# Query projections, VectorE priorities and dummy products in the head of a one-core transformer block

## The chip, the cores and the metric

The kernel runs on one core of a Trainium2 chip. The metric is device time in microseconds (us). The runs of one kernel scatter by a few us. A ratio is the mean time of one kernel's runs over the mean of the other's runs of the same rounds, with a 95% interval, so it is not quite the ratio of the medians that are quoted.

In this kernel TensorE multiplies matrices (15918 products before the change), ScalarE computes exponentials and tanh (1024 and 112), and VectorE (1498 instructions) copies results out of PSUM, adds and normalises. "Span" is the length of the profiled execution. It is about 2 us shorter than the time of the same run (before: 1158.1 and 1159.92 us).

## The reference, cut to what matters

```python
# x: 2048 x 1024, 32 heads of 32, one shared key/value head, FFN width 3584
mod = (silu(c) @ w_mod).reshape(...)             # six vectors of 1024: sa, ca, ga, sb, cb, gb
h = layernorm(x) * (1 + ca) + sa
q, k, v = h @ wq, h @ wk, h @ wv                 # softmax(q k' / sqrt(32)) @ v, then @ wo
x = x + ga * attention(h)
h = layernorm(x) * (1 + cb) + sb
x = x + gb * ((silu(h @ w1) * (h @ w3)) @ w2)
```

## The kernel before

The program is a list of nodes with dependencies. A list scheduler in the kernel file places them when it is built, using its own estimates of durations, and then writes one fixed instruction order for each engine. Queries are worked on in 8 blocks of 256. For each of 8 groups of 4 heads, a "score group" (line 915) writes scores for 256 keys, and two exponentials (line 925) read them. P·V (line 975) and row sums (line 1002) follow. The FFN of the block before fills TensorE between score groups. For the first block only, the projections of head groups 0 to 3 (`HEAD = 4`) and half of the keys are done first, so that exponentials can start early. This beginning is called the head below.

```python
# the scheduler's choice among ready nodes: lowest key first
if e == "pe":                                    # TensorE
    def key(c):
        s, n = c
        if n.cls == "S":   r = 0                 # score groups
        elif n.cls is not None: r = 1 if att or t - n.est > 1.0 else 4     # P·V, row sums
        else:              r = 3 if n.prio >= 4 else 0.5
        return (r, n.prio, n.seq)
elif e == "dve":                                 # VectorE
    def key(c):
        s, n = c
        p = n.prio
        if t - n.est > 4.0: p -= 3
        return (p, n.seq)

# "warm": if the schedule sees TensorE idle before 250 us, it inserts k dummy products
gap = s - t_free[e] - 0.3 - (0.1 if mode != "F" else 0.0) - (0.1 if n.mode != "F" else 0.0)
k = int(gap / self.warm[1])

def ln(t):                                       # layer norm of one tile of 128 tokens
    (ln_stats_act if t in ONACT else ln_stats)(t)        # ln_stats has priority 2 - bp
    ln_scale(t, 1)
    ln_norm(t, t, en="pool" if t in ONPOOL else "dve")   # priority 2 - bp, bp = 0

# transposes of norm tiles have priority TRP = 1; a projection's default is prio=5
kproj(0, 256, (2, 3, 4, 5, 6, 7))                # third argument: allowed PSUM banks
qproj(0, 256, 0, (2, 3, 4, 5, 6, 7), prio=1)
kproj(256, 256, (2, 3, 4, 5, 6, 7))
kproj(512, 512, (1,))
...
qproj(0, 256, 1, (0, 1))
vproj(0, (0, 1))
vproj(1, (0, 1))
for f in range(2, HEAD):
    qproj(0, 256, f, (0, 1))
tr(8, 4, (0, 1))                                 # transposes of tiles 8 to 11
for t in range(12, 16):
    ln(t)
... # cut
# attention: score group i uses four of the six score banks, which are banks 2 to 7
parts = [(0, 2, 2 * ((2 * i) % 3), 2), (2, 2, 2 * ((2 * i + 1) % 3), 2)]
```

The softmax here doesn't subtract the row's maximum and nothing guards it: scores larger than these inputs give would overflow.

## Time and profile before

| | before |
|---|---|
| time, median of the first 3 runs | 1160.13 us (1158.57 to 1160.46) |
| span of the profiled run | 1158.1 us |
| first exponential | 29.2 us |
| ScalarE idle for scores, 28 to 130 us | 12.3 us, of which 0.5 is before the first exponential |
| last score group starts | 1044.7 us |
| from there to the end ("tail") | 113.4 us |

First come the busy times by stretch: from:to, length, busy us of TensorE (PE), its weight loads (PEld), VectorE (DVE), ScalarE (ACT) and GpSimd with instruction counts, then TensorE's granted clock, the DMA share and GB/s.

```profile
18.50:25.30 6.80, 6.71 (x114) 6.00 (x115) 1.88 (x4) 4.05 (x9) 0.00 (x0) 0.50 1.07 364
39.00:46.00 7.00, 5.67 (x104) 3.63 (x106) 6.01 (x18) 5.97 (x7) 4.08 (x10) 0.51 0.41 117
46.00:60.00 14.00, 11.16 (x261) 8.29 (x254) 11.27 (x34) 9.27 (x10) 0.99 (x2) 1.00 0.34 89
600.00:700.00 100.00, 99.60 (x1407) 67.44 (x1406) 94.25 (x137) 99.88 (x115) 1.73 (x2) 1.00 0.63 177
```

In the middle (600 to 700 us) ScalarE is hardly ever idle (99.88 of 100 us). In the head it is: between 46 and 60 us it works 9.3 of 14 us. Twice the clock is granted at half (0.50 and 0.51 in the first two stretches). Finer stretches put the two half-clock intervals at 18.5 to 25.3 us and 39.0 to 45.8 us, 6.8 us each. Why the clock falls there is not shown.

ScalarE's idle times in the head, from its timeline: start, us, what ran, and in brackets the idle time before it and what ended that.

```profile
29.21 3.83 ACT L925 ACTIVATE UREG<-SP 128x1024 bf16<-128x1024 f32 x4 [0.49 <-PE SP L915]
35.60 7.44 ACT L925 ACTIVATE UREG<-SP 128x1024 bf16<-128x1024 f32 x8 [2.56 <-PE SP L915]
43.80 1.94 ACT L925 ACTIVATE UREG<-SP 128x1024 bf16<-128x1024 f32 x2 [0.76 <-PE SP L915]
47.02 9.27 ACT L925 ACTIVATE UREG<-SP 128x1024 bf16<-128x1024 f32 x10 [1.29 <-PE SP L915]
61.86 13.44 ACT L925 ACTIVATE UREG<-SP 128x1024 bf16<-128x1024 f32 x14 [5.57 <-PE SP L915]
```

The longest, 5.57 us, is explained by TensorE's own timeline: after the score group at 53.60 it transposes, does two rounds of P·V and row sums, and only then the fourth query projection (59.67), which the score group at 61.41 needs.

```profile
53.60 0.40 PE L915 MATMUL SP<-QT,KT 32*128 32x256 bf16 x8 [0.77 <-ACT UREG L925]
...
56.06 1.06 PE L975 MATMUL PB<-UREG,V 128*32 128x256 bf16 x32
56.95 1.05 PE L1002 MATMUL PB<-UREG,SEL 128*32 128x256 bf16 x32
57.82 1.04 PE L975 MATMUL PB<-UREG,V 128*32 128x256 bf16 x32
...
58.69 1.05 PE L1002 MATMUL PB<-UREG,SEL 128*32 128x256 bf16 x32
59.67 1.05 PE L658 MATMUL PB<-HREG,WREG 128*128 128x256 bf16 x8
...
61.41 0.40 PE L915 MATMUL SP<-QT,KT 32*128 32x256 bf16 x8
```

A projection has rank 3 on TensorE (priority 5), a transpose rank 0.5 (priority 1). Norms that VectorE finishes early make transposes ready, and these pass the fourth projection (`f = 3`).

The third projection (`f = 2`) was late before any of these transposes (the first runs at 48.52 us). It needs a PSUM bank (projections and values share banks 0 and 1), and VectorE emptied the values (line 651) only at 40.52 us, after norm statistics (line 530):

```profile
37.57 2.46 DVE L530 BATCH_NORM_STATS2 ST<-X 128x6 f32<-128x512 bf16 x4
40.52 0.44 DVE L651 TENSOR_TENSOR V<-PB,VB 128x128 bf16<-128x128 f32 x2
41.76 1.44 PE L658 MATMUL PB<-HREG,WREG 128*128 128x256 bf16 x6
```

The cause is the ageing rule in the cut above: work that has waited for over 4 us gets 3 points off its priority, so an aged norm (2 - 3 = -1) passes an evacuation (1).

The chain of work that ended last, by engine:

```profile
PE 92%; ACT 3%; DVE 3%; DMA 1%; SPq 1%; issue 0%; POOL 0%; DVEq 0%
```

This is not to be read as "TensorE alone is the limit". In the middle TensorE and ScalarE are both busy almost all the time (99.60 and 99.88 us of the 100 us from 600 to 700), and the chain follows one of them by hairs.

### The profile page before, as it was taken

The page shows a single profiled execution, that of the slowest core. Times are in us where ns is not written, and L with a number is a line of the kernel's source. Part 1 is how long each engine was busy: PE and PEld are TensorE (multiplying, and loading weights), DVE is VectorE, ACT ScalarE, POOL GpSimd, SP SyncE. Part 2 cuts the span into 40 slices and gives each one's busy share as a digit, 9 for nine tenths or more (in the row PEclk, how much of TensorE's full clock was granted, in tenths as well). Part 3 has the DMA queues.
Part 4 walks back from the last instruction along what each step waited for, and adds up shares of the span by engine and source line. Part 5 has one row for each costly group of instructions (what it writes and reads, how often), then busy time and mean ns, then how long its engine had stood idle before and what let it go on. Part 6 is the DMA issues. An engine that isn't in the chain of part 4 may idle for free.

```text
span 1158.1 us, 35702 instructions
## 1 busy us (share of the span) xinstructions
PE 1122.6 (97%) x15918; PEld 767.1 (66%) x15918; DVE 984.7 (85%) x1498; ACT 1027.6 (89%) x1170; POOL 43.5 (4%) x86
## 2 busy tenths in 40 slices
PE   7799998999979999999999999999999999999998
PEld 6564444776646766777577766776677766777887
DVE  5837889999888999899999998999989999997452
ACT  5789999999999999999999999999999999992110
POOL 3200001000000001000100001000100010000000
PEclk8899999999989999999999999999999999999999
DMA  9337005956546565856496567766586649756996
GB/s 331 113 129 220 19 2 127 275 169 178 166 122 190 169 193 149 248 170 192 119 279 196 159 177 194 226 169 174 152 252 181 185 122 258 204 152 192 284 291 160
DMA packets 385417, 211.10 MB, mean 182 GB/s; under 512 B 21744, under 2 KB 376048, under 8 KB 385264
## 3 DMA queue, kind: packets, MB, share of 16 engines
q1 hardware_dynamic: 383184, 208.69, 64.5%
q8 instruction: 125, 2.05, 0.8%
q10 hardware_dynamic: 2080, 0.13, 0.1%
q14 instruction: 28, 0.23, 0.1%
HBM read 201.46 MB, written 4.19 MB: 178 GB/s over the span
## 4 chain that ended last, share of the span: by engine, by line
PE 92%; ACT 3%; DVE 3%; DMA 1%; SPq 1%; issue 0%; POOL 0%; DVEq 0%
PE PB L1141 33%; PE PB L1175 16%; PE SP L915 14%; PE PB L975 11%; PE PB L1107 5%; PE PB L658 4%; PE SP L1141 3%; ACT UREG L925 3%; PE SP L1175 2%; PE PB L1002 2%; DMA UREG<-in_w_mod_dram 1%; PE PB L637 1%; PE PB L838 0%; PE SP L1107 0%; DVE WO L850 0%
## 5 line engine op out<-in xcount | busy, mean ns | idle before, releaser
L925 ACT ACTIVATE UREG<-SP 128x1024 bf16<-128x1024 f32 x1024 | 968.6, 1075 | 18.8 <-PE SP L915 16.4
L948 DVE TENSOR_TENSOR UREG<-UREG 128x2048 bf16<-128x2048 bf16 x240 | 292.8, 1220 | 12.8 <-ACT UREG L925 10.8
L915 PE MATMUL SP<-QT,KT 32*128 32x256 bf16 x4096 | 204.8, 274 | 16.0 <-ACT UREG L925 15.0
L1141 PE MATMUL PB<-QT,WREG 128*128 128x256 bf16 x1648 | 207.4, 274 | 1.8 <-DVE DSB L1026 1.6
L1141 PEld LDWEIGHTS PB<-QT,WREG 128*128 128x128 bf16 x1648 | 150.1, 98 | 46.8 <-issue 31.2
L942 DVE TENSOR_TENSOR UREG<-UREG 128x2048 bf16<-128x2048 bf16 x120 | 146.4, 1220 | 11.5 <-PE PB L1002 6.4
L915 PEld LDWEIGHTS SP<-QT,KT 32*128 32x128 bf16 x4096 | 61.2, 93 | 138.6 <-ACT UREG L925 79.6
L1141 PE MATMUL PB<-QT,HREG 128*128 128x256 bf16 x1056 | 133.7, 274 | 0.8 <-DVE DSB L1026 0.8
L975 PE MATMUL PB<-UREG,V 128*32 128x256 bf16 x4032 | 132.2, 277 | 1.7 <-DVE QT L610 0.9
L975 PEld LDWEIGHTS PB<-UREG,V 128*32 128x32 bf16 x4032 | 99.3, 98 | 27.5 <-issue 17.9
L1141 PEld LDWEIGHTS PB<-QT,HREG 128*128 128x128 bf16 x1056 | 96.1, 98 | 29.7 <-issue 19.6
L1175 PE MATMUL PB<-WREG,HREG 128*128 128x256 bf16 x812 | 101.2, 273 | 0.0
L1175 PEld LDWEIGHTS PB<-WREG,HREG 128*128 128x128 bf16 x812 | 75.3, 98 | 20.4 <-issue 11.4
L1175 PE MATMUL PB<-HREG 128*128 128x256 bf16 x532 | 67.8, 274 | 0.0
L1141 PE MATMUL PB<-QT,X 128*128 128x256 bf16 x528 | 67.8, 274 | 0.0
L658 PE MATMUL PB<-HREG,WREG 128*128 128x512 bf16 (+1 forms) x312 | 64.1, 343 | 0.3 <-DVE DSB L1026 0.3
L957 DVE TENSOR_TENSOR UREG<-UREG 128x2048 bf16<-128x2048 bf16 x52 | 63.4, 1220 | 0.5
L1150 ACT ACTIVATE GSB<-GSB 128x512 bf16<-128x512 bf16 x56 | 38.8, 693 | 27.5 <-DVE GSB L1148 27.5
L1014 DVE COPY XN<-PB 128x256 f32<-128x256 f32 x63 | 26.6, 422 | 39.6 <-PE PB L1002 39.3
L1175 PEld LDWEIGHTS PB<-HREG 128*128 128x128 bf16 x532 | 49.2, 98 | 14.3 <-issue 8.0
L1107 PE MATMUL PB<-WO,QT 128*128 128x512 bf16 x232 | 57.6, 381 | 0.2 <-DVE QT L661 0.2
L1141 PEld LDWEIGHTS PB<-QT,X 128*128 128x128 bf16 x528 | 48.2, 98 | 14.3 <-issue 9.3
(139 smaller groups left out, 1031.9 us busy)
## 6 DMA issues: line engine op xcount, KB each, us to landing
WREG<-in_B_w_dram SPq DMA_DIRECT2D x112, 512.0 KB, 5.1
HREG<-in_B_w_dram SPq DMA_DIRECT2D x74, 512.0 KB, 5.2
WREG<-in_B_w_dram SPq DMA_DIRECT2D x33, 896.0 KB, 5.1
X<-in_B_w_dram SPq DMA_DIRECT2D x38, 512.0 KB, 5.1
HREG<-in_B_w_dram SPq DMA_DIRECT2D x21, 896.0 KB, 5.2
X<-in_B_w_dram SPq DMA_DIRECT2D x10, 896.0 KB, 5.1
X<-in_A_x_dram SPq DMA_DIRECT2D x32, 256.0 KB, 5.0
WREG<-in_w_mod_dram SPq DMA_DIRECT2D x16, 512.0 KB, 4.7
```

The costliest lines, as they stand in the source:

```text
L658: g = mm_group(NC, lambda e, b, c: e.matmul(b[:, 0:n], WQ[:, c, f * P:(f + 1) * P], HT[:, c, sl], start=c == 0, stop=c == NC - 1), lambda ...
L915: r = e.matmul(SP[:, b, o:o + qn], KT[32 * gg:32 * gg + 32, kts[j] * P:(kts[j] + 1) * P], QT[32 * gg:32 * gg + 32, f, q0:q0 + qn], start=T ...
L925: G.add("act", lambda e, u=u, h0=h0, n=n, b0=b0, nb=nb: e.activation(U[:, u, h0 * W:(h0 + n) * W].rearrange("p (b w) -> p b w", b=nb), SP[ ...
L942: G.add("dve", lambda e, tr=tr, u=u, fu=first_u: e.tensor_tensor(TR[:, tr, 0:4 * W], U[:, fu, 0:4 * W], U[:, u, 0:4 * W], ALU.add), reads= ...
L948: G.add("dve", lambda e, tr=tr, u=u: e.tensor_tensor(TR[:, tr, 0:4 * W], TR[:, tr, 0:4 * W], U[:, u, 0:4 * W], ALU.add), reads=[("TR", tr) ...
L957: G.add("dve", lambda e, ta=ta, tb=tb: e.tensor_tensor(TR[:, ta, 0:4 * W], TR[:, ta, 0:4 * W], TR[:, tb, 0:4 * W], ALU.add), reads=[("TR", ...
L975: r = e.matmul(PB[g.bank][32 * gg:32 * gg + 32, 0:qn], V[:, kt, :], U[:, pu, (gg * npk + j) * qn:(gg * npk + j + 1) * qn], start=w0 + n == ...
L1014: G.add("dve", lambda e, g=g, f=f: e.tensor_copy(ASB[:, f % 4, 0:qn], PB[g.bank][:, 0:qn]), writes=[("ASB", f % 4), ("XN", 2 + f % 4 // 2) ...
L1107: g = mm_group(NC, lambda e, b, f, t=t, h=h: e.matmul(b, QT[:, f, t * P:(t + 1) * P], WO[:, f, h * 512:(h + 1) * 512], start=f == 0, stop= ...
L1141: return e.matmul(b[:, j * qn:(j + 1) * qn], w13[:, w, c, j * P:(j + 1) * P], QT[:, c, q0:q0 + qn], start=c == 0, stop=c == NC - 1)
L1150: G.add("act", lambda e, b=b: e.activation(TB[b], GS[b], ACT.Tanh, scale=0.5), reads=[("GS", b)], writes=[("TB", b)], clear=alias("TB") if ...
L1175: G.add("pe", lambda e, g=g, j=j, fc=fc, hf=hf, first=first, w2s=w2s: e.matmul(PB[g.bank][:, j * 256:(j + 1) * 256], HHT[:, hf * NH + fc, ...
```

## The change

The intent is to have the queries of the first four head groups earlier, to let VectorE empty PSUM before it works on norms that are not yet needed, and to keep TensorE's clock up in the first 26 us (it was granted at 0.50 from 18.5 to 25.3 us). That the new dummies do this was my assumption.

```diff
-                gap = s - t_free[e] - 0.3 - (0.1 if mode != "F" else 0.0) - ...
+                gap = s - t_free[e] - (0.05 if t < self.warm[4] else 0.3) - (0.1 if mode != "F" else 0.0) - ...
@@ vproj: evacuation of the values
-              writes=[("V", tb)], groups=[(g, "r")], dur=dve_t(128), prio=1)
+              writes=[("V", tb)], groups=[(g, "r")], dur=dve_t(128), prio=-4)
@@ qproj: evacuation of the queries
-              writes=qkeys(f, t0, n), ..., prio=-5 if t0 == f == 0 else 1)
+              writes=qkeys(f, t0, n), ..., prio=-5 if t0 == 0 and f < HEAD else 1)
@@ ln
-        (ln_stats_act if t in ONACT else ln_stats)(t)
+        bp = -3 if t >= 8 else 0
+        if t in ONACT:
+            ln_stats_act(t)
+        else:
+            ln_stats(t, bp=bp)
         ln_scale(t, 1)
-        ln_norm(t, t, en="pool" if t in ONPOOL else "dve")
+        ln_norm(t, t, en="pool" if t in ONPOOL else "dve", bp=bp)
@@ sequence and banks
-    kproj(0, 256, (2, 3, 4, 5, 6, 7))
-    qproj(0, 256, 0, (2, 3, 4, 5, 6, 7), prio=1)
-    kproj(256, 256, (2, 3, 4, 5, 6, 7))
-    kproj(512, 512, (1,))
+    kproj(0, 256, (2, 3, 4, 5))
+    qproj(0, 256, 0, (2, 3, 4, 5), prio=1)
+    kproj(256, 256, (6, 7))
+    kproj(512, 512, (6, 7))
 ... # cut
-    qproj(0, 256, 1, (0, 1))
+    qproj(0, 256, 1, (0, 1), prio=1)
     vproj(0, (0, 1))
+    qproj(0, 256, 2, (0, 1), prio=1)
     vproj(1, (0, 1))
-    for f in range(2, HEAD):
-        qproj(0, 256, f, (0, 1))
+    for f in range(3, HEAD):
+        qproj(0, 256, f, (0, 1), prio=1)
@@ dummies: 128 columns become 512
-                r = e.matmul(PB[b][:, 0:P], IDENT[:], IDENT[:], ...)
+                r = e.matmul(PB[b], IDENT[:], IDENT[:].unsqueeze(1).broadcast_to([P, 4, P]), ...)
-    G.warm = (WARM, P / 2400.0 + 0.0026, warm, ident)
+    G.warm = (WARM, MM, warm, ident, 26.0)
```

The change has three parts, named below by what they are: the **sequence** (with its banks), the **priorities** on VectorE and the **dummies**.

(The diff is shortened.)

More of the change, by code (lines that the diff above doesn't have):

```diff
@@ L227, in schedule @@
             if e == "pe" and self.warm is not None and t < self.warm[0]:
-                gap = s - t_free[e] - 0.3 - (0.1 if mode != "F" else 0.0) - (0.1 if n.mode != "F" else 0.0)
+                gap = s - t_free[e] - (0.05 if t < self.warm[4] else 0.3) - (0.1 if mode != "F" else 0.0) - (0.1 if n.mode != "F" else 0.0)
                 fb = [x for x in free_banks() if x[0] + SEM_LAT <= t_free[e]]
@@ L662, in qproj @@
               reads=[("BIA", 0 if f == 0 else 1 if f < HEAD else 2)],
-              writes=qkeys(f, t0, n), groups=[(g, "r")], dur=dve_t(n), prio=-5 if t0 == f == 0 else 1)
+              writes=qkeys(f, t0, n), groups=[(g, "r")], dur=dve_t(n), prio=-5 if t0 == 0 and f < HEAD else 1)
     def qkeys(f, q0, qn):
@@ L1215, in f @@
             for _ in range(k):
-                r = e.matmul(PB[b][:, 0:P], IDENT[:], IDENT[:], start=True, stop=True, skip_group_check=True)
+                r = e.matmul(PB[b], IDENT[:], IDENT[:].unsqueeze(1).broadcast_to([P, 4, P]), start=True, stop=True, skip_group_check=True)
             return r
         return f
-    G.warm = (WARM, P / 2400.0 + 0.0026, warm, ident)
+    G.warm = (WARM, MM, warm, ident, 26.0)
     span = G.schedule(range(8))
```

## The prediction

> **What bounds the kernel now.** From its first exponential (29.2 us, timeline) to its last (about 1041 us) ScalarE sets the pace: in the stretches table it is 99.5% busy in nearly every 100 us between 200 and 1000, one exponential of 128x1024 each 0.93 us, 1024 of them, plus about 0.46 us for each of 98 tanh. Between two score groups (1.86 us) TensorE has 1.75 us of work (0.33 us of scores, 13 products of 0.109 us). After the last score TensorE alone works for about 117 us (450 L1141, 448 L1175 and the last block). So 29.2 + 952 + 45 + 12 (ScalarE idle in the head) + 117 = 1155, against a span of 1158.
>
> The change touches only the first 62 us directly. There, by the waits and the timeline, ScalarE idles four times between exponentials: 2.56 us (33.0), 0.76 (43.0), 1.29 (45.7) and 5.57 (56.3): 10.2 us in all. The last is TensorE doing transposes, P·V and row sums of two groups (3.9 us) and only then the fourth query projection, which the next score needs. The clock was granted at half from 18.5 to 25.3 and from 39.0 to 45.8.
>
> **What it does, from the instruction order.**
> 1. Query projections 1 to 3 come before score groups 3, 5 and 6 instead of 3, 8 and 13; their evacuations pass the norms on VectorE. Summing the trace's durations over the new TensorE order, the 7.0 us between score groups 12 and 13 disappears; no later gap of the head exceeds 2.5 us. The waits of 0.76, 1.29 and 5.57 us should fall to under 1 us together: -7 us.
> 2. It costs something: the key projections of 512 columns now sit in score banks. The second score group comes after 28 key products, query projection 1 and half the first values: 4.25 us after the first, where ScalarE has 1.86 us of work. I expect a ScalarE wait of about 2.3 us near 31 us, about what the old 2.56 us was (1.4 us of which was TensorE stopped in mid-group with nothing to wait for).
> 3. Dummies: 133 of 128 columns become 54 of 512. The first run takes the same time (56x128 against 15x512 columns). In 15.1 to 18.5 they add only about 0.2 us of streaming. [...]both half-clock stretches here are 6.8 us[...]. Whether 0.2 us tips it at 18.5 I hold for even odds. If it does, 0 to 1.3 us is gained before the first exponential, because w_mod still arrives at DMA pace to 21 us or later. Expected: -0.5 us. The second cold stretch should vanish[...].
> 4. One tanh less precedes the last exponential: -0.5 us.
> 5. Given back: FFN work is reordered too. After the last score 482 first-FFN products remain instead of 450, 32 x 0.109 = +3.5 us in the tail where only TensorE works.
>
> Sum: -7 -0.2 -0.5 -0.5 +3.5 = about -4.7 us.
>
> **Prediction: 1155.5 us, 1150 to 1160 us.** Faster by over 2%: 0.01; within: 0.98; slower: 0.01.
>
> **Right if** ScalarE's idle time on scores between 28 and 130 us falls from 12.3 to about 5 us, its longest wait is the second score group's, first exponential within 1.5 us of 29.2, last exponential 7 to 9 us earlier, and the stretch from last score to end is 3 to 4 us longer.
>
> **Wrong if** VectorE is late with the tighter evacuations so that TensorE's fixed order stalls; if the mid-group stop moves into a score's path; if a cold stretch appears elsewhere; or if the tail is not purely TensorE's, so that the 3.5 us does not return.

## The result, and the profile after

The changed kernel took 1155.89 us (median of 6, 1155.31 to 1157.44) beside 1159.47 us for the kernel before (6 runs). The ratio is 0.9972, interval [0.9959, 0.9984]: faster, by a third of a per cent. Line numbers move by five: 915 is now 920, 925 is 930, 1175 is 1180.

The same stretches after:

```profile
18.50:25.30 6.80, 6.17 (x166) 4.76 (x164) 2.05 (x8) 4.59 (x11) 0.83 (x1) 1.00 1.06 363
39.00:46.00 7.00, 5.30 (x104) 2.62 (x104) 7.00 (x20) 7.00 (x9) 2.31 (x6) 1.00 0.51 143
46.00:60.00 14.00, 12.00 (x260) 7.69 (x256) 9.00 (x25) 14.00 (x16) 1.44 (x4) 1.00 0.91 299
600.00:700.00 100.00, 99.05 (x1407) 67.48 (x1404) 94.59 (x138) 99.59 (x114) 2.24 (x4) 1.00 0.64 178
```

In this profile the clock stays up (1.00 from 13 to 55 us), and ScalarE is busy without a break from 39 to 60 us. Its timeline now has one long wait:

```profile
27.79 1.91 ACT L930 ACTIVATE UREG<-SP 128x1024 bf16<-128x1024 f32 x2
33.66 29.51 ACT L930 ACTIVATE UREG<-SP 128x1024 bf16<-128x1024 f32 x32 [3.96 <-PE SP L920]
63.54 1.94 ACT L930 ACTIVATE UREG<-SP 128x1024 bf16<-128x1024 f32 x2 [0.37 <-PE SP L920]
65.72 9.43 ACT L930 ACTIVATE UREG<-SP 128x1024 bf16<-128x1024 f32 x10 [0.25 <-PE SP L920]
```

That wait stands before the second score group, as predicted, but it is longer: 3.96 us instead of 2.3. Between the first score group (27.03 us) and the second (33.21 us) TensorE stopped for 1.24 us in the middle of a group, with nothing to wait for ("issue"):

```profile
27.36 0.39 PE L637 MATMUL SP<-HREG,WKS 128*32 128x512 bf16 x1
28.99 0.40 PE L637 MATMUL SP<-HREG,WKS 128*32 128x512 bf16 x3 [1.24 <-issue]
```

The other end of the kernel shows what was given back. Here are the last score group and TensorE's last group, before:

```profile
1044.74 0.40 PE L915 MATMUL SP<-QT,KT 32*128 32x256 bf16 x8
1147.42 6.28 PE L1175 MATMUL PB<-WREG,HREG 128*128 128x256 bf16 x56
```

and after:

```profile
1036.41 0.40 PE L920 MATMUL SP<-QT,KT 32*128 32x256 bf16 x8
1142.81 6.28 PE L1180 MATMUL SP<-WREG,HREG 128*128 128x256 bf16 x56
```

The last score group comes 8.3 us earlier (1044.74 - 1036.41). From there to the end of the span it is 1158.1 - 1044.74 = 113.4 us before and 1153.5 - 1036.41 = 117.1 us after, so 3.7 us go back. 8.3 - 3.7 = 4.6 us is the difference of the spans.

The chain of work that ended last has changed sides, although the time fell by a third of a per cent only:

```profile
PE 46%; ACT 45%; DVE 6%; issue 1%; SPq 1%; DMA 1%; POOL 0%
```

### The profile page after: what moved, and what is told of

It reads as the page before. It is cut to its first block, busy times and chain, and to the rows that moved or that the text cites. A ratio compares the mean times of both kernels' runs of the same rounds, so it can differ in the third digit from the quotient of the medians.

```text
span 1153.5 us, 35455 instructions
## 1 busy us (share of the span) xinstructions
PE 1119.9 (97%) x15839; PEld 762.4 (66%) x15839; DVE 989.5 (86%) x1498; ACT 1026.0 (89%) x1170; POOL 39.0 (3%) x86
## 4 chain that ended last, share of the span: by engine, by line
PE 46%; ACT 45%; DVE 6%; issue 1%; SPq 1%; DMA 1%; POOL 0%
ACT UREG L930 41%; PE PB L1180 12%; PE SP L920 6%; PE PB L1146 5%; PE PB L980 5%; PE PB L658 4%; PE PB L1112 4%; PE SP L1180 4%; PE SP L1146 3%; ACT WREG L1155 2%; ACT GSB L1155 2%; DVE UREG L953 1%; DVE UREG L947 1%; PE PB L1007 1%; DMA UREG<-in_w_mod_dram 1%
## 5 line engine op out<-in xcount | busy, mean ns | idle before, releaser
L1146 PE MATMUL PB<-QT,WREG 128*128 128x256 bf16 x1632 | 203.1, 273 | 0.6 <-DVE DSB L1031 0.2
L1146 PEld LDWEIGHTS PB<-QT,WREG 128*128 128x128 bf16 x1632 | 148.9, 98 | 44.7 <-issue 28.5
L980 PE MATMUL PB<-UREG,V 128*32 128x256 bf16 x4096 | 127.4, 273 | 0.7 <-ACT UREG L930 0.5
L1180 PE MATMUL PB<-WREG,HREG 128*128 128x256 bf16 x728 | 92.6, 273 | 1.9 <-DVE HREG L1158 1.9
L1180 PEld LDWEIGHTS PB<-WREG,HREG 128*128 128x128 bf16 x728 | 66.9, 98 | 23.5 <-issue 13.8
L1146 PEld LDWEIGHTS PB<-QT,X 128*128 128x128 bf16 x544 | 50.3, 98 | 13.2 <-issue 7.8
L1180 PE MATMUL PB<-HREG 128*128 128x256 bf16 x448 | 57.3, 273 | 1.3 <-DVE HREG L1158 1.3
L1155 ACT ACTIVATE WREG<-WREG 128x512 bf16<-128x512 bf16 x56 | 40.1, 715 | 20.5 <-DVE WREG L1153 20.5
L1180 PEld LDWEIGHTS PB<-HREG 128*128 128x128 bf16 x448 | 41.0, 98 | 14.5 <-issue 8.9
```

The costliest lines, as they stand in the source:

```text
L980: r = e.matmul(PB[g.bank][32 * gg:32 * gg + 32, 0:qn], V[:, kt, :], U[:, pu, (gg * npk + j) * qn:(gg * npk + j + 1) * qn], start=w0 + n == ...
L1146: return e.matmul(b[:, j * qn:(j + 1) * qn], w13[:, w, c, j * P:(j + 1) * P], QT[:, c, q0:q0 + qn], start=c == 0, stop=c == NC - 1)
L1155: G.add("act", lambda e, b=b: e.activation(TB[b], GS[b], ACT.Tanh, scale=0.5), reads=[("GS", b)], writes=[("TB", b)], clear=alias("TB") if ...
L1180: G.add("pe", lambda e, g=g, j=j, fc=fc, hf=hf, first=first, w2s=w2s: e.matmul(PB[g.bank][:, j * 256:(j + 1) * 256], HHT[:, hf * NH + fc, ...
```

## The experiments

All kernels gave correct results. Each experiment was timed in 4 to 6 runs, the kernel before in 9 to 11. "Ledger" in the expectations means the prediction's way of summing gains and losses; a "cold stretch" is one at half clock (granted 0.50). Each call measured its own runs of the kernel before: medians 1160.47, 1160.74 and 1160.65 us in the three calls. So compare the ratios, not the medians.

One table for all profiled runs. "Waits" are ScalarE's idle times that a score group ended: those from the first exponential to 130 us, and those after 130 us. The tail is the span minus the start of the last score group. All times are in us.

| kernel | ratio to before, interval | first exp | waits to 130 | waits later | last score | tail |
|---|---|---|---|---|---|---|
| before | 1 | 29.2 | 11.8 | 4.2 | 1044.7 | 113.4 |
| the change | 0.9972 [0.9959, 0.9984] | 27.8 | 5.2 | 5.6 | 1036.4 | 117.1 |
| warm_only | 0.9990 [0.9978, 1.0003] | 27.5 | 11.1 | 3.9 | 1042.0 | 113.4 |
| no_warm | 0.9970 [0.9957, 0.9982] | 31.2 | 4.6 | 4.6 | 1038.7 | 117.1 |
| order_only | 1.0057 [1.0043, 1.0071] | 31.0 | 13.4 | 6.9 | 1049.2 | 117.1 |
| evac_only | 0.9971 [0.9959, 0.9984] | 29.8 | 4.9 | 5.4 | 1038.1 | 117.1 |
| evac_warm | 0.9958 [0.9940, 0.9975] | 28.5 | 6.4 | 6.0 | 1038.7 | 117.1 |
| order_warm | 1.0034 [1.0014, 1.0053] | 27.6 | 11.8 | 6.5 | 1043.9 | 117.1 |
| after_vq | 1.0014 [0.9998, 1.0029] | 27.6 | 10.6 | 6.0 | 1042.8 | 117.1 |
| kbank | 0.9958 [0.9943, 0.9974] | 28.1 | 6.7 | 5.4 | 1038.3 | 117.1 |
| after_wide | 0.9951 [0.9937, 0.9966] | 28.9 | 4.1 | 5.6 | 1036.5 | 117.0 |
| after_close | 0.9961 [0.9945, 0.9977] | 27.7 | 7.0 | 5.6 | 1038.1 | 117.1 |
| evac_warm_rate09 | 1.0253 [1.0233, 1.0273] | 27.7 | 6.7 | 21.6 | 1079.9 | 107.4 |
| ew_rate064 | 0.9953 [0.9938, 0.9968] | 28.5 | 4.2 | 7.6 | 1041.6 | 111.7 |

### One part alone, and one part taken away

**warm_only**: before, with only the dummies of the change.

```diff
-gap = s - t_free[e] - 0.3 - ...          # and dummies of 128 columns
+gap = s - t_free[e] - (0.05 if t < self.warm[4] else 0.3) - ...   # and dummies of 512 columns
```

> The kernel before with only the new dummies (512 columns, closer together until 26 us); the order of real work is that of before. Ledger theory: only the first exponential moves, from 29.2 to about 27.8 us, because the clock no longer falls at 18.5 us; ScalarE's waits on scores between 28 and 130 us stay near 12 us with the 5.6 us one among them, because that one is TensorE's order; the tail after the last score stays 113.4 us. Time 1158.0 us (-1.4). Rival 'the clock did it': the long wait shrinks with the clock too, and the time falls to about 1156, all of the gain. Rival 'luck of the DMA': the clock still falls at 18.5 us and nothing changes (1159.5).

It took 1159.66 us (1157.25 to 1160.97). The first exponential came at 27.5 us, and the clock did not fall at 18.5 us (1.00 from 18.5 to 25.3 us). The long wait stayed at 5.57 us, to the hundredth, so it is TensorE's order and not its clock. The new dummies alone bought 0.1% (ratio 0.9990), which is within noise. "The clock did it" is refuted.

**no_warm**: the change with the old dummies.

```diff
-gap = s - t_free[e] - (0.05 if t < self.warm[4] else 0.3) - ...   # and dummies of 512 columns
+gap = s - t_free[e] - 0.3 - ...          # and dummies of 128 columns
```

> The changed kernel with the old dummies back (128 columns, old margin). Ledger theory: first exponential back at about 29.2 us, half clock at 18.5 to 25.3 us as before; waits on scores between 28 and 130 us near 5 us as in the changed kernel; tail 117 us. Time 1157.3 us (+1.4 over the changed kernel). Rival 'the clock did it': near 1159.5, all of the gain lost. Rival 'luck of the DMA': clock stays up, first exponential near 27.8, 1155.9.

It took 1157.35 us (1155.5 to 1159.03), as the ledger said, and the ratio is that of the whole change. The clock was at half (0.50) between 20.5 and 31 us, for about 10 us this time, and the first exponential came only at 31.2 us. But ScalarE then waited 2.61 us instead of 3.96 for its second score group, and there was no stop in mid-group. Part of what the earlier start gains is lost again in the next wait.

**order_only**: before, with the sequence and its banks only.

```diff
-qproj(0, 256, 1, (0, 1)); vproj(0, (0, 1)); vproj(1, (0, 1)); for f in range(2, HEAD): qproj(0, 256, f, (0, 1))
+qproj(1, prio=1); vproj(0); qproj(2, prio=1); vproj(1); qproj(3, prio=1)   # and the key projections in banks (6, 7)
```

> The kernel before with only the new sequence of projections and their new banks; priorities on VectorE and dummies as before. From its TensorE order: the 7.0 us between score groups 12 and 13 is gone, the 4.3 us before group 2 is there, tail 482 + 448 products (+3.5 us). Ledger theory, either part alone removes the long wait: waits on scores in 28 to 130 us about 5 to 6 us, the longest about 4 us at group 2; first exponential 29.2; tail 117; time about 1157.3. Rival 'VectorE priority did it': the long wait stays over 4 us, evacuations still stand behind norms, time 1159 or more (with the longer tail up to 1163).

It took 1166.93 us (1166.16 to 1168.65), 0.57% slower than before and 9.6 us over what I expected. The built order has no gap of 7 us, and no wait on scores is longer than 2.99 us. Yet the waits to 130 us add up to 13.4 us, more than before. The longest (2.99 us) and the third longest (1.73 us) stand right behind stops of TensorE in mid-group:

```profile
63.88 0.94 PE L976 MATMUL PB<-UREG,V 128*32 128x256 bf16 x27 [0.98 <-issue]
...
66.84 0.94 PE L1003 MATMUL PB<-UREG,SEL 128*32 128x256 bf16 x28
70.33 0.29 PE L1003 MATMUL PB<-UREG,SEL 128*32 128x256 bf16 x4 [2.55 <-issue]
70.56 0.40 PE L916 MATMUL SP<-QT,KT 32*128 32x256 bf16 x8
```

Twenty-eight of the 32 products of one row-sum group run, nothing happens for 2.55 us, and the last four follow. ScalarE then waits 2.99 us. Against before, this span is 8.1 us longer: 1.8 from a later first exponential (half clock from about 20 to 30 us), 3.7 from the longer tail, and the rest (8.1 - 1.8 - 3.7 = 2.6) between the two.

**evac_only**: before, with the priorities only.

```diff
 prio of value and query evacuations: 1 -> -4 / -5
+bp = -3 if t >= 8 else 0        # norm statistics and norms of tiles 8 to 15: priority 2 -> 5
```

> The kernel before with only the priorities on VectorE (evacuations ahead of norms, late norms ahead of other work); sequence, banks and dummies as before. From its TensorE order: no gap of 7.0 us AND none of 4.3 us before group 2 (largest 2.5); tail 482 + 448 products. Ledger theory: waits on scores in 28 to 130 us about 3.5 us, first exponential 29.2, tail 117, time about 1155.5, as good as the whole change although the clock still falls at 18.5 us. Rival 'the sequence did it': long wait stays, time 1159 or more.

It took 1157.04 us (1156.67 to 1158.24), ratio 0.9971: all of the gain of the whole change, without the sequence and without the dummies. "The sequence did it" is refuted. ScalarE's waits of 2.56, 0.76, 1.29 and 5.57 us have become these:

```profile
29.78 3.82 ACT L929 ACTIVATE UREG<-SP 128x1024 bf16<-128x1024 f32 x4 [0.72 <-PE SP L919]
34.78 7.56 ACT L929 ACTIVATE UREG<-SP 128x1024 bf16<-128x1024 f32 x8 [1.19 <-PE SP L919]
42.92 20.27 ACT L929 ACTIVATE UREG<-SP 128x1024 bf16<-128x1024 f32 x22 [0.57 <-PE SP L919]
63.55 1.94 ACT L929 ACTIVATE UREG<-SP 128x1024 bf16<-128x1024 f32 x2 [0.36 <-PE SP L919]
```

VectorE's order tells how. The norms of tiles 8 to 15 now have priority 5, so even an aged one (5 - 3 = 2) stays behind an evacuation, and the values leave PSUM at 36.2 and 37.6 us instead of 40.5:

```profile
36.17 0.27 DVE L651 TENSOR_TENSOR V<-PB,VB 128x128 bf16<-128x128 f32 x1
37.56 0.27 DVE L651 TENSOR_TENSOR V<-PB,VB 128x128 bf16<-128x128 f32 x1
38.43 1.59 PE L658 MATMUL PB<-HREG,WREG 128*128 128x256 bf16 x13
```

So the banks are free, and query projections 2 and 3 stand before score groups 5 to 7 instead of 7 to 13, long before the first transposes (48.06 us). If only the `bp` line is changed and the evacuations keep priority 1, the program is the same, byte for byte. The same holds for the whole change: take its raised evacuation priorities out, and nothing changes. So two of the three priorities do nothing once the norms step back, and the gain of evac_only is that of the `bp` line alone. The reverse was built too, but not run: with the evacuations raised and the norms left alone, the schedule has the projections just as early. What else the `bp` line does is seen in after_vq below.

**evac_warm**: the change without the sequence.

```diff
-# sequence and banks of the change
+# sequence and banks of before
```

> The whole change without its new sequence and banks: VectorE priorities and new dummies only. Theory 'the sequence is not needed': no 4.3 us before score group 2, first exponential near 27.6 us with the clock up, waits on scores in 28 to 130 us about 4 us, tail 117 us; 1154.5 us, as good as the whole change or 1 us better. Rival 'the sequence carries part of the gain': 1157 us or more, waits over 6 us.

It took 1156.77 us (1152.53 to 1158.02), ratio 0.9958. It is not to be told from the whole change, and no worse. The sequence is not needed. The waits were 6.4 us where I expected 4: in this profile the clock was at half (0.50) from 31 to 35 us, and a stop of 1.3 us fell into the key projections.

**order_warm**: before with sequence and dummies, the last corner of the eight.

```diff
-# sequence, banks and dummies of before
+# sequence, banks and dummies of the change; priorities of before
```

> The kernel before with the new sequence and banks and the new dummies, VectorE priorities of before: the last corner of the three parts. Theory 'order_only lost by late clock and two mid-group stops of TensorE (3.5 us)[...]': first exponential 27.7 instead of 31.0, no or shorter stops, 1159 to 1162 us. Rival 'the sequence without the new priorities is slow by itself': stops again or waits on evacuations over 8 us between 50 and 130 us, 1164 us or more.

It took 1164.26 us (1160.94 to 1167.32), inside the rival's range: slow again, although the first exponential came at 27.6 us. One stop of 1.62 us (at 68 us) and waits of 1.81 and 1.12 us follow each other around 70 us.

**after_vq**: the change without the line that lets the norms step back.

```diff
-        bp = -3 if t >= 8 else 0
+        bp = 0
```

> The changed kernel without the lowered priority of the late norms; the raised evacuations of values and queries stay. (With the norms lowered, the raised evacuations change no engine's instruction order at all.) Theory 'it is the norms stepping back that matters': VectorE is late with evacuations between 45 and 75 us, waits on scores in 24 to 130 us over 8 us, 1159 us or more. Rival 'either way of putting evacuations first serves': waits about 5 us, 1156 us.

It took 1161.81 us (1160.42 to 1164.94), ratio 1.0014: the whole gain is gone, with the raised evacuations, the sequence and the dummies still in. The waits to 130 us are 10.6 us instead of 5.2. But the cause that I had written down is not what the trace shows: VectorE is not late with evacuations of values, keys or queries (no wait of TensorE on one lasts over 0.34 us between 24 and 130 us), and the queries of the first four head groups are ready as early as in the change (the last is emptied at 38.35 us, in the change at 38.65). Up to 57 us the only wait on scores that the view lists is the one before group 2, 3.87 us (3.96 in the change). What is lost is lost later, 6.7 us of waits against 1.2:

```profile
62.34 3.77 ACT L926 ACTIVATE UREG<-SP 128x1024 bf16<-128x1024 f32 x4 [0.91 <-PE SP L916]
67.60 7.44 ACT L926 ACTIVATE UREG<-SP 128x1024 bf16<-128x1024 f32 x8 [1.49 <-PE SP L916]
102.47 9.27 ACT L926 ACTIVATE UREG<-SP 128x1024 bf16<-128x1024 f32 x10 [1.82 <-PE SP L916]
112.67 7.58 ACT L926 ACTIVATE UREG<-SP 128x1024 bf16<-128x1024 f32 x8 [0.93 <-PE SP L916]
```

The first two stand near TensorE's stops of 0.93 us (61 us) and 1.08 us (67 us); the last two (2.75 us) do not stand behind a stop. So early projections are not enough: the `bp` line also changes what TensorE does between 57 and 113 us, and no run here isolates what of it counts.

What the three kernels without that line but with the sequence (order_only, order_warm, after_vq) have in common, and the changed kernel and evac_only do not: VectorE scales the last query weights (line 744) later (done at 50.6 to 53.3 us instead of 41.8 and 44.0 us), so their buffer is free later, and the 2 MB load of `wo` into it is issued right then, at 50.6 to 53.3 us instead of 41.8 and 44.0 us. All three have stops of TensorE between 61 and 71 us, the fast ones none over 0.3 us there. Whether the later loads cause the stops is not settled: the kernel before issues the same load at 57.8 us, and has no such stop after it.

### The banks

**kbank**: the change with the key projections in the banks of before.

```diff
-    kproj(256, 256, (6, 7)); kproj(512, 512, (6, 7))
+    kproj(256, 256, (2, 3, 4, 5, 6, 7)); kproj(512, 512, (1,))
```

> The changed kernel with the key projections back in the banks of before: the score banks are free for group 2, so 1.7 us instead of 4.3 us of work stands before it (2.5 us before group 3). Tail (482 + 448 products) and dummies are those of the changed kernel. Theory 'the banks cost about 2 us of ScalarE wait': the longest wait on scores in 24 to 130 us falls from about 4 to about 2 us, last score 1 to 2 us earlier, 1154.5 us. Rival 'the wait is only moved to group 3 with TensorE's mid-group stop': waits in sum unchanged at 5 us, 1155.9 us.

It took 1156.13 us (1153.83 to 1157.22), ratio 0.9958, not to be told from the change. The wait of 3.96 us before group 2 became 1.50 us before group 2 and 2.07 us before group 3: in sum nearly the same. Moving the banks back moves the wait; the keys of group 3 have to be projected in any case.

### Which side of the dummies

**after_wide**: wide dummies, old margin.

```diff
-gap = s - t_free[e] - (0.05 if t < self.warm[4] else 0.3) - ...
+gap = s - t_free[e] - 0.3 - ...
```

> The changed kernel with dummies 512 wide but the old margin: one dummy instead of two at each of the three places between 15 and 20 us (0.2 us of streaming less in each). Theory [...]: the clock falls near 19 us as with the old dummies, first exponential 29 us or later, 1157.4 us. Rival 'width alone is enough': no half clock, first exponential 27.8, 1155.9 us.

It took 1155.26 us (1155.0 to 1156.57), ratio 0.9951. The clock did fall to half, but for about 3.5 us only (21.5 to about 25 us), and the first exponential came at 28.9 us. Half of what I expected happened: the clock fell, the time did not suffer.

**after_close**: narrow dummies, new margin.

```diff
-    matmul of 512 columns, two at a time
+    matmul of 128 columns, eight at a time
```

> The changed kernel with dummies 128 wide but the new margin: eight of 128 columns (1024 columns) where the change has two of 512 (1024 columns). Theory 'streamed columns count, not their width': the clock stays up, first exponential 27.8, 1155.9 us. Rival 'width counts[...]': the clock falls near 19 us, first exponential 29 us or later, 1157.4 us.

It took 1156.97 us (1155.69 to 1158.14), ratio 0.9961. There was no half clock before 30 us, and the first exponential came at 27.7 us. In this profile as many columns at a quarter of the width went with the same result. One profile each is thin evidence: ew_rate064 below has the wide dummies and the new margin, and its clock was still at half from 21.5 to 25 us. Here the clock was at half from 30 to 34 us, and the wait before group 2 grew to 5.75 us.

Taken together: in the four profiles with the old narrow dummies at the old margin (before, no_warm, order_only, evac_only) the clock fell to 0.50 between 18.5 and 21 us, and the first exponential came at 29.2 to 31.2 us. In the nine with the new margin, the change included, the clock did not fall before 21.5 us (in eight of them not before 30 us), and it came at 27.5 to 28.5 us. That is 30.3 against 27.9 us in the mean. In the time it is hard to find. The four pairs that differ by the dummies alone change by -0.10% (before), -0.13% (priorities), -0.23% (sequence) and +0.02% (both) of the time of before, and each ratio has an interval of about +-0.13 to 0.2%. So a gain from the dummies is not shown.

### Two tries at a better version

The tail holds FFN products that the schedule could have put between score groups. Both kernels below change only the schedule's belief about an exponential's length, on top of evac_warm.

**evac_warm_rate09**

```diff
-    return n / 1200.0 + 0.057
+    return n / 1200.0 + 0.09
```

> A try at a better version: evac_warm with the schedule's assumed cost of one exponential raised by 33 ns (0.91 to 0.943 us; the trace shows 0.93), so that it puts 14 instead of 13 FFN products between score groups. From its order 396 + 448 products remain after the last score, not 482 + 448: 86 x 0.109 = 9.4 us less tail, 107.7 us. Theory 'the tail is leftover FFN work that fits into TensorE's slack': waits on scores grow by 2 us at most, 1147 us. Rival 'there is no slack, TensorE is the limit in the middle too': waits on scores between 130 us and the last exponential grow by 8 us or more and the time stays near 1154.5 us.

It took 1190.09 us (1189.15 to 1193.27), 2.5% slower. The tail shrank as computed, to 107.4 us. But the last score group came at 1079.9 us, 41 us later than in evac_warm, and both theories missed the time. From 130 us to its last exponential ScalarE is idle for 30.9 us instead of 8.1: the waits on scores that the view lists are 21.6 us in 42 pieces instead of 6.0, the rest is too short to be listed. The other 18 us stand as busy time of ScalarE (920.8 us instead of 902.4), and why is not shown. TensorE's own waits after 130 us, longest first:

```profile
PE SP L919 <- ACT UREG L929: 16.4, 26, 1.4
PE PB L1145 <- DVE QT L1128: 11.3, 6, 2.0
```

The second line is the new one: FFN products (line 1145) that now stand earlier wait for the transposed norms of their block (line 1128), six times, up to 2.0 us. In evac_warm that wait was 0.3 us in all.

**ew_rate064**

```diff
-    return n / 1200.0 + 0.057
+    return n / 1200.0 + 0.064
```

> A milder try at a better version: evac_warm with the schedule's assumed cost of one exponential raised by only 7 ns (13 products stay in most gaps). From its order 435 + 448 products remain after the last score, 47 fewer than in the changed kernel: 5.1 us less tail, 112 us. Theory 'a few more products fit': waits on scores after 130 us stay under 8 us, 1152 us. Rival 'FFN work put earlier meets norms and transposed tiles that are not there yet, as in evac_warm_rate09': TensorE waits for L1128's tiles over 6 us, last score 5 us or more later, 1157 us or more.

It took 1155.59 us (1152.5 to 1156.46), ratio 0.9953. This lies between what the theory (1152) and the rival (1157 or more) said. Against evac_warm, on which it builds, the tail is 5.4 us shorter (111.7) and the last score group 2.9 us later (1041.6), but the ratios (0.9953 and 0.9958) cannot be told apart. It is among the fastest, but its interval overlaps those of evac_warm, kbank and the change, so no version here is shown to beat the change.

## Why the prediction was right

The time: 1155.5 us was predicted with a range of 1150 to 1160, and 1155.89 measured. The range also holds the kernel before (1159.47), so the time alone tests little; the points below do. The fall was predicted as 4.7 us; the medians fell by 3.6 us, the spans by 4.6 us. Point by point:

1. **The waits in the head.** Predicted: the waits of 0.76, 1.29 and 5.57 us fall to under 1 us together, 12.3 us become about 5. Measured: 5.2 us, and beside the second group's wait 5.2 - 3.96 = 1.2 us in all. Right in size. Right, too, that TensorE's order was the cause and not its clock: warm_only kept the 5.57 us. What the prediction did not see is which part did it. It took the earlier projections and the evacuations as one step. evac_only has the whole gain alone. after_vq, with everything but the norms stepping back, has the projections just as early and lacks the 5.57 us wait, as the prediction reasons, and yet gains nothing, because other waits come after 57 us. That the change keeps these to 1.2 us was no part of the prediction's argument. (The trace has projections 1 to 3 right before score groups 2, 3 and 5, not 3, 5 and 6.)
2. **The new wait before score group 2.** Predicted 2.3 us, measured 3.96 us. Of the 1.7 us too much, 1.24 us are the stop in mid-group; in no_warm, without a stop, the wait was 2.61 us. "The mid-group stop moves into a score's path" stands in the prediction under "Wrong if". It happened, and other terms made up for it.
3. **The clock at 18.5 us.** Even odds, and -0.5 us. It stayed up (1.00), and the first exponential came 1.4 us earlier than in that profile of before, 2.4 us in the mean of the profiles. The term was too small at the first exponential, but the time shows little of it, so the sum was not spoiled. The second cold stretch did vanish in this profile, but not for good: evac_warm, kbank and after_close had a cold stretch (0.50) of about 3.5 us between 30 and 35 us.
4. **The tail.** Predicted +3.5 us from 32 products of 0.109 us, measured +3.7 us, and the same 117 us in every kernel with that order. This is the term that a look at the head alone would have missed. Without it the sum would have been -8.2 us.
5. **The last exponential** was to start 7 to 9 us earlier. It started at 1046.6 us before and at 1038.3 us after, 8.3 us earlier.

The sum was met in part by luck. To the last exponential the prediction had -8.2 us and the trace has -8.3, but the parts differ: ScalarE's idle time between its first and last exponential fell by 5.1 us (18.3 to 13.2) and not by 7.2, mainly because the waits after 130 us grew from 4.2 to 5.6 us and a tanh wait of 0.4 us came in, which no term had. The first exponential was 1.4 us earlier and not 0.5, and ScalarE's busy time in between was 1.7 us less (999.1 to 997.4) where 0.5 was expected for one tanh less; why the rest of it fell is not shown.

For order_only the same way of reckoning was 9.6 us off. Summing durations over the new order found every gap that the order contains, but the stops in mid-group (0.98 and 2.55 us) and the cold stretches (about 20 to 30 and 40 to 44 us) are not in the order. They hit this kernel in the path of the scores more than the changed one, whose one stop cost 1.24 us.

## What to carry to other kernels

When a list scheduler fixes the order, compare the built orders before timing, end to end: the gain of this change stood in the head, 3.7 of 8.3 us were given back 1000 us later in the tail, and two of its priorities changed no instruction at all. Split a change with several parts into all its corners; here one line (late norms step back) carried the gain, and another part (the sequence) was a loss in order_only and order_warm, where that line was missing. Work that seems to fit into an engine's slack between two waits may have inputs that are not ready yet: moving 86 FFN products forward shortened the tail by 10 us and cost 41.

## What the traces here leave open

- What sets the clock. Half-clock stretches (0.50) lasted about 3.5 us (warm_only, 39.5 to 42.9 us), 6.8 us (before, 18.5 to 25.3 us) and 10 us (no_warm, 20.5 to 31 us) here. How much work keeps the clock up is not shown: 3.83 to 4.37 us of busy TensorE between 13.0 and 18.5 us were followed by a fall at 18.5 to 21 us (before, order_only, no_warm, evac_only), 4.63 us by none at that place (the change, warm_only). But ew_rate064 had 4.89 us and a fall at 21.5 us, so no threshold follows. In before, TensorE's longest wait in that stretch was 0.95 us.
- What the stops in mid-group are. TensorE stopped for 0.9 to 2.6 us in the middle of a group with nothing to wait for, in nine of the fourteen kernels between 27 and 33 us, and in order_only, order_warm and after_vq between 61 and 71 us. The DMA engines were full in the change's stop (a share of 104% by the view, 27.75 to 28.99 us) but 7.5% busy in the longest (order_only, 67.78 to 70.33 us). No run here shows the cause.
- What becomes of time when an engine is kept from waiting and another, nearly as busy, takes over as the limit. The chain here went from 92% TensorE to 46% TensorE and 45% ScalarE with a third of a per cent of time.
